# A retention, channel-MLP and attention kernel: other first transfers, matmuls on a constant, and a last value product in halves

## The chip, the cores and the metric

The kernel runs on one core of one Trainium2 chip. The metric is the device time of one execution in microseconds (us), lower is better. The engines are called as the profile calls them: PE is TensorE (PEld its weight loads), ACT is ScalarE, DVE is VectorE, POOL is GpSimd and SP is SyncE, which issues the DMAs.

## The reference, cut

```python
B, H, S, D = 2, 8, 768, 64           # batch, heads, tokens, head width; model width 512
# 1 retention: a decaying state per head
for t in range(S):
    state = gamma * state + outer(k[:, :, t], v[:, :, t])
    y[:, :, t] = q[:, :, t] @ state / sqrt(D)
# 2 channel MLP on the heads put side by side (width 512, hidden 2048)
xn = (x - mean) / sqrt(var + 1e-6) * g_ln
x = x + relu(xn @ w_ch1) @ w_ch2
# 3 four causal attentions of width 64; each token takes its best two by a gate
for e in range(4):
    q, k, v = x @ wq[e], x @ wk[e], x @ wv[e]
    ye = softmax(causal(q @ k.T / 8)) @ v @ wo[e]
    out += (weight of e for the token, or 0) * ye
```

## The kernel before

**Stages.** The tokens of a batch are cut into six tiles of 128, so the retention stage has twelve tiles, taken in the order batch 0, batch 1, batch 0 and so on (`tiles`). The channel stage walks eight blocks `f` of 256 hidden columns, in six of which (`SEVEN`) it forms sums of weights and of activations and multiplies with those (`w_sums`, `m_h7`); its second product is L594, whose results VectorE adds to the residual stream at L597. The attention stage follows (`q_phase`, `a_phase`), for pairs of query tiles `g`.

**One retention tile** (`r_tile`). `load` brings two pairs: `kq`, keys and queries with the head width on the partitions, and `vk`, values and keys with tokens on the partitions, 512 KB each, and for batch 0 a table `tabY` of 256 KB. GpSimd scales the values by the table `tabV` (L414, result `vs`). TensorE makes the scores (L426), VectorE masks them with `caus` (L430, result `am`), TensorE multiplies the masked scores with `vs` (L445), adds the part of the state from the third tile on (L438), and updates the state from `vk` and `vs` (L452), which ScalarE copies to SBUF (L459). The result times `tabY` is transposed with the identity `ident` (L470), normalised and transposed back.

**What sets the order.** Every step is a node of a planner (`Plan`): the engine or engines it may run on with a planned cost, what it reads and writes, and a priority, which is the order of creation plus a bias. `issue` walks planned time: at each moment it looks at the engines in turn and gives a free one the ready step with the lowest priority number whose buffers fit, and that order is what each engine gets. A DMA is a step of the engine "D" and is issued by SyncE, in planned order. A buffer is given the first free place of its kind in planned time (there are four for `kq`, three for `vk`), and on the chip the DMA waits until that place is really free. The two rules in the code:

```python
free = {e: 0.0 for n in self.nodes for e in n.eng}   # engines in the order of first mention
...
for e in free:
    if free[e] > t:
        continue
    for n in sorted(waiting[e], key=lambda n: n.prio):
```

**The end.** For a query tile pair `g` and an expert pair `p`, `a_value` transposes the weighted softmax rows (L879), copies them (L333, where every copy that either ScalarE or VectorE may do is recorded) and multiplies them with the values (L890) for both query tiles at once, 256 columns; ScalarE and VectorE make a high and a low part `at` of it (L896, L897). `a_out` multiplies these with `wo` (L909), six terms per query tile `z`, copies the sums out and writes them (L918). For the last pair the second query tile leaves in two halves that share a bank.

Of the kernel before, what the change touches and what calls it, by code (L numbers as in the profile page):

```python
# [27 lines left out]
AF = mybir.ActivationFunctionType  # L28
OP = mybir.AluOpType
# [3 lines left out]
B, H, S, D = 2, 8, 768, 64  # L33
DM = H * D
FF = 4 * DM
E, HD = 4, 64
C = 128
# [11 lines left out]
NEG = -1000000000.0  # L49
# [162 lines left out]
def retention_channel_mlp_mixture_attention(ctx: ExitStack, tc: tile.TileContext, a):  # L212
    nc = tc.nc
    pe, act, dve, pool, sp = nc.tensor, nc.scalar, nc.vector, nc.gpsimd, nc.sync
# [6 lines left out]
    caus = cst.tile([128, C], F32, name="caus")  # L221
    tabV = cst.tile([128, NC, H], F32, name="tabV")
# [4 lines left out]
    negs = cst.tile([128, C], F32, name="negs")  # L227
    ps = pp.tile([128, 8 * 512], F32, name="ps")
# [27 lines left out]
    f32, f32r, u32 = typed(F32), typed(F32R), typed(U32)  # L256
# [11 lines left out]
    x = o_r  # L268
# [21 lines left out]
    x = o_h - 2 * (4 * KB + 16)  # L290
# [20 lines left out]
    P = Plan()  # L311

    def new(n):
        return Buf(PL[n], n)

    def PE(c, fn, r=(), w=(), hold=()):
        P.add({"T": c}, lambda e: fn(), r, w, lat=0.2, hold=hold)

    def ACT(c, fn, r=(), w=()):
        P.add({"A": c}, lambda e: fn(), r, w)  # L320

    def DVE(c, fn, r=(), w=()):
        P.add({"V": c}, lambda e: fn(), r, w)
# [14 lines left out]
    def act_c(n):  # L338
        return 0.06 + n * 0.84e-3

    def dve_c(n):
        return 0.08 + n * 1.05e-3
# [21 lines left out]
    TY = {}  # L364
# [4 lines left out]
    def load(i):  # L369
        b, c = tiles[i]  # L370
        kq, vk = new("kq"), new("vk")
        n = 2 if i == 0 else 1
        for y in range(n):
            h = slice(1024 // n * y, 1024 // n * (y + 1))
            DMA(512e3 / n, lambda h=h: sp.dma_start(f32(kq)[:, h], a["kq"][b, c][:, h]), w=[(kq, y)])
            if i == 0 and y == 0:
                DMA(24e3, lambda: sp.dma_start(tabV, a["tabV"]), w=["tabV"])
                DMA(64e3, lambda: sp.dma_start(caus, a["caus"]), w=["caus"])
        DMA(512e3, lambda: sp.dma_start(f32(vk), a["vk"][b, c]), w=[vk])
        if b == 0:  # L380
            ty = TY[c] = new("tabY")
            DMA(256e3, lambda: sp.dma_start(f32(ty), a["tabY"][c]), w=[ty])
        L[i] = (kq, vk)

    load(0)
    DMA(64e3, lambda: sp.dma_start(ident, a["ident"]), w=["ident"])
    load(1)
    load(2)
    DMA(2e3, lambda: sp.dma_start(gln, a["gln"]), w=["gln"])
    DVE(0.1, lambda: dve.memset(half, -0.5), w=["half"])  # L390
# [8 lines left out]
    STATE = new("state")  # L399
# [6 lines left out]
    def r_tile(i):  # L406
# [6 lines left out]
        vs = new("vs")  # L413
        POOL(1.15, lambda: pool.tensor_tensor(h3(f32(vs)), h3(v()),  # L414
                                             tabV[:, c, :, None].to_broadcast([128, H, D]), OP.mult),
             r=[vk, "tabV"], w=[vs])
        if c < 2:
            zero_s(SNB[b][c])
        PA, AM = [new("ps") for _ in range(2)], [new("am") for _ in range(2)]
# [28 lines left out]
        if c < NC - 1:  # L448
            def upd():
                for p in range(NP):  # L450
                    for h in range(2):
                        pe.matmul(state(b)[64 * h:64 * h + 64, p * D:(p + 1) * D], lhsT=h3(k())[:, 2 * p + h],  # L452
                                  rhs=h3(f32(vs))[:, 2 * p + h], start=(i == 0 and p == 0), stop=False,
                                  skip_group_check=True)
            PE(0.65, upd, r=[vk, vs] + (["first"] if i == 1 else []), w=[(STATE, b)] + (["first"] if i == 0 else []))
            sn = SN[b] = SNB[b][c % 2]
            for h in range(2):
                hs = slice(64 * h, 64 * h + 64)
                ACT(0.38, lambda h=h, hs=hs: act.activation(  # L459
                    r4(f32(sn))[hs, :, hs], state(b)[hs].rearrange("p (a e) -> p a e", a=NP), AF.Copy),  # L460
                    r=[(STATE, b)], w=[(sn, h)])
# [242 lines left out]
    MW = {}  # L704
# [10 lines left out]
    def mw(n, lo, k, c0, c1):  # L715
        h, l, w = MW[n]
        return f32r(l if lo else h)[:, k * w + c0:k * w + c1]
# [144 lines left out]
        P.bias += (20, 40)[b]  # L862
        return PR

    def a_value(b, g, p, PRS):
# [17 lines left out]
        av = new("psa")  # L883
        for j0 in range(0, nj, 2):
            def mm(j0=j0):
                for j in (j0, j0 + 1):
                    last = j == nj - 1
                    for x in range(2):
                        e = 2 * p + x
                        pe.matmul(f32(av)[64 * x:64 * x + 64, (C if last else 0):2 * C],  # L890
                                  lhsT=f32(VV[b, j])[:, e * HD:(e + 1) * HD],
                                  rhs=f32(PT[x])[:, 2 * j * C:(2 * j + (1 if last else 2)) * C],
                                  start=(j == 0), stop=last, skip_group_check=True)
            PE(0.97 if j0 + 2 < nj else 0.76, mm, r=[VV[b, j0], VV[b, j0 + 1]] + [(pt, j0 // 2) for pt in PT], w=[av])
        at = new("at")
        ACT(act_c(256), lambda: act.activation(f32r(at)[:, :256], f32(av, 256), AF.Copy), r=[av], w=[(at, 0)])  # L896
        DVE(dve_c(256), lambda: dve.tensor_tensor(f32r(at)[:, 256:], f32(av, 256), f32(at)[:, :256], OP.subtract),  # L897
            r=[av, (at, 0)], w=[(at, 1)])
        return at

    def a_out(b, g, ats, last):
        terms = [(p, y, lo) for p in range(2) for y, lo in ((0, 0), (0, 1), (1, 0))]
        pas, obs = [new("psa") for _ in range(2)], [new("ob") for _ in range(2)]

        def part(z, i0, i1, cs):
            def mm():
                for i in range(i0, i1):
                    p, y, lo = terms[i]
                    pe.matmul(f32(pas[z])[:, cs], lhsT=f32r(ats[p])[:, y * 256 + z * C:y * 256 + (z + 1) * C],  # L909
                              rhs=mw("wo", lo, p, cs.start, cs.stop), start=(i == 0), stop=(i == 5),  # L910
                              skip_group_check=True)
            PE(0.22 * (i1 - i0) * (cs.stop - cs.start) / DM, mm,
               r=list(MW["wo"][:2]) + [(ats[p], y) for p, y, lo in terms[i0:i1]], w=[pas[z]])

        def leave(z, cs):
            t0 = (2 * g + z) * C
            COPY(cs.stop - cs.start, lambda: f32(obs[z])[:, cs], lambda: f32(pas[z])[:, cs], [pas[z]], [(obs[z], cs.start)])
# [3 lines left out]
        all_ = slice(0, DM)  # L921
        if last:
            for i0, i1 in ((0, 3), (3, 5)):
                for z in range(2):
                    part(z, i0, i1, all_)
        for z in range(2):
            for cs in (slice(0, DM // 2), slice(DM // 2, DM)) if last and z else (all_,):
                part(z, 5 if last else 0, 6, cs)
                leave(z, cs)

    pieces = [(f, i) for f in range(NFC) for i in ((2, 3, 0, 1) if f in SEVEN else range(NPC))]
    early = {0: (0, 1), 2: (2, 3), 7: (4, 5), 9: (6, 7)}
# [133 lines left out]
```

## Time and profile before

| | us |
|---|---|
| median of three runs | 459.22 (459.13 to 460.65) |
| the profiled execution | 459.39 |
| its span, first to last instruction | 457.3 |
| TensorE busy | 442.7 (97%) |
| VectorE, ScalarE, GpSimd busy | 336.1, 228.4, 208.8 |
| data moved | 40.09 MB |

Times in the views below run from the span's start. A busy time of TensorE includes the pipelined ends of its matmuls. A product of plain float32 operands stands in the trace as two instructions, one that is made of rounded halves as one. "Idle before" in brackets is how long the engine stood still ahead of a row, and what released it.

### The profile page before, as it was taken

How to read it: one execution, taken by the hardware profiler on the slowest of the kernel's cores; microseconds unless marked ns; L12 is line 12 of the kernel's file. 1: busy time of each engine (PE TensorE's matmuls, PEld its weight loads, DVE VectorE, ACT ScalarE, POOL GpSimd, SP SyncE). 2: the span in 40 equal slices, each digit the busy share in tenths (PEclk: the TensorE clock that was granted, in tenths of full speed). 3: DMA queues.
4: the chain of work that ended last, by engine and by line, in shares of the span. 5: the costliest groups of instructions: out<-in, count | busy, mean ns of one | idle time of the engine just before them, and what ended most of it. 6: DMA issues, size and time to landing. Idle time of an engine off the chain costs nothing.

```text
span 457.3 us, 8243 instructions
## 1 busy us (share of the span) xinstructions
PE 442.7 (97%) x3081; PEld 417.1 (91%) x3081; DVE 336.1 (73%) x701; ACT 228.4 (50%) x479; POOL 208.8 (46%) x212
## 2 busy tenths in 40 slices
PE   4999999999999999999999999999999999999996
PEld 3888899999999999999999999999899988898774
DVE  2697885779848959879779677466657988778962
ACT  0686684365246326244354154145534767745852
POOL 1588779879976304323244044007500415224450
PEclk9999999999999999999999999999999999999999
DMA  7899930224103104014022002002220221101111
GB/s 264 315 326 326 345 100 6 94 97 134 46 1 138 48 0 162 24 36 149 1 72 68 1 2 92 1 0 94 69 70 16 63 62 47 47 1 46 49 48 46
DMA packets 14984, 40.09 MB, mean 88 GB/s; under 512 B 2272, under 2 KB 4960, under 8 KB 14944
## 3 DMA queue, kind: packets, MB, share of 16 engines
q1 hardware_dynamic: 14944, 39.57, 25.5%
q8 instruction: 24, 0.39, 0.3%
q14 instruction: 16, 0.13, 0.1%
HBM read 33.27 MB, written 3.15 MB: 80 GB/s over the span
## 4 chain that ended last, share of the span: by engine, by line
PE 80%; DVE 5%; DMA 5%; ACT 3%; issue 3%; POOL 2%; SPq 0%; POOLq 0%; DVEq 0%; ACTq 0%
PE ps L594 25%; PE ps L653 15%; PE ps L575 7%; PE ps L737 6%; PE ps L890 4%; PE ps L879 4%; PE ps L774 4%; PE ps L909 4%; DMA kq<-in_kq_dram 3%; PE ps L837 2%; PE ps L838 2%; DVE sf L546 2%; PE ps L445 2%; PE ps L426 2%; PE ps L470 2%
## 5 line engine op out<-in xcount | busy, mean ns | idle before, releaser
L594 PE MATMUL ps<-h,w 128*128 128x384 f32 x768 | 145.9, 336 | 1.7 <-DVE xT L597 1.4
L594 PEld LDWEIGHTS ps<-h,w 128*128 128x128 f32 x768 | 133.9, 188 | 3.3 <-DVE xT L597 2.7
L597 DVE TENSOR_TENSOR xT<-xT,ps 128x384 f32<-128x384 f32 x128 | 69.3, 550 | 29.1 <-PE ps L594 28.9
L859 POOL TENSOR_SCALAR pr<-pr,sm,gate 128x384 f32<-128x384 f32 (+5 forms) x48 | 34.8, 734 | 81.2 <-DVE ps L844 32.5
L531 POOL TENSOR_TENSOR w<-wy,w 128x512 fp32r<-128x512 f32 x26 | 34.4, 1333 | 56.2 <-PE ps L594 34.8
L653 PE MATMUL ps<-t,S 128*128 128x384 f32 x216 | 43.3, 335 | 0.0
L847 ACT ACTIVATE pr<-ps,sm 128x384 f32<-128x384 f32 (+5 forms) x48 | 30.3, 634 | 16.5 <-DVE sm L845 10.4
L653 PEld LDWEIGHTS ps<-t,S 128*128 128x128 f32 x216 | 38.0, 188 | 0.0
L660 ACT ACTIVATE u<-ps 128x384 f32<-128x384 f32 x36 | 17.5, 487 | 37.8 <-PE ps L653 31.0
L575 PE MATMUL ps<-x,w 128*128 128x384 f32 x192 | 35.0, 336 | 0.0
L506 ACT ACTIVATE wx<-raw 128x512 f32<-128x512 f32 x32 | 21.5, 671 | 23.9 <-DVE ps L510 16.2
L575 PEld LDWEIGHTS ps<-x,w 128*128 128x128 f32 x192 | 33.3, 188 | 0.0
L507 POOL TENSOR_SCALAR wx<-wx 128x512 f32<-128x512 f32 x32 | 20.5, 641 | 26.7 <-ACT wx L506 25.7
L845 DVE TENSOR_REDUCE sm<-ps 128x1 f32<-128x384 f32 (+5 forms) x48 | 30.0, 625 | 2.8
L653 PE MATMUL ps<-x,w 128*128 128x384 f32 x144 | 28.8, 335 | 0.0
L530 ACT ACTIVATE w<-wy 128x512 fp32r<-128x512 f32 x26 | 16.2, 628 | 24.1 <-PE ps L594 18.6
L668 ACT ACTIVATE h<-ps 128x384 fp32r<-128x384 f32 x36 | 17.6, 488 | 18.8 <-PE ps L653 9.4
L653 PEld LDWEIGHTS ps<-x,w 128*128 128x128 f32 x144 | 25.3, 188 | 0.0
L669 DVE SCALAR_TENSOR_TENSOR h<-ps,h 128x384 fp32r<-128x384 f32 x36 | 19.9, 552 | 4.8 <-ACT h L668 4.8
L512 DVE SCALAR_TENSOR_TENSOR wy<-raw,ps 128x512 uint32<-128x512 uint32 x32 | 21.7, 683 | 2.3 <-POOL w L531 1.8
L510 DVE SCALAR_TENSOR_TENSOR ps<-wx,ps 128x512 uint32<-128x512 uint32 x32 | 22.2, 695 | 1.0
L508 DVE TENSOR_SCALAR ps<-wx 128x512 uint32<-128x512 uint32 x32 | 22.0, 688 | 0.8 <-POOL wx L507 0.3
(116 smaller groups left out, 885.2 us busy)
## 6 DMA issues: line engine op xcount, KB each, us to landing
raw<-in_w_dram SPq DMA_DIRECT2D x32, 512.0 KB, 4.0
vk<-in_vk_dram SPq DMA_DIRECT2D x12, 512.0 KB, 5.6
kq<-in_kq_dram SPq DMA_DIRECT2D x11, 512.0 KB, 6.2
qk<-qk SPq DMA_DIRECT2D x32, 96.0 KB, 2.1
out_dram<-ob SPq DMA_DIRECT2D x11, 256.0 KB, 2.0
tabY<-in_tabY_dram SPq DMA_DIRECT2D x6, 256.0 KB, 5.2
vraw<-in_wv_dram SPq DMA_DIRECT2D x1, 520.0 KB, 3.6
kq<-in_kq_dram SPq DMA_DIRECT2D x2, 256.0 KB, 3.0
```

Of the source, the lines that this page charges most:

```text
L508: DVE(0.62, lambda: dve.tensor_scalar(u32(z), u32(x), 4, 1, op0=OP.logical_shift_left, op1=OP.logical_shift_right), r=[x], w=[z])
L510: DVE(0.7, lambda: dve.scalar_tensor_tensor(u32(z), u32(x), 0x80000000, u32(z), op0=OP.bitwise_and, op1=OP.bitwise_or), r=[x, z], w=[z])
L512: DVE(0.7, lambda: dve.scalar_tensor_tensor(u32(y), words(0), 29, u32(z), op0=OP.logical_shift_right, op1=OP.bitwise_or), r=[raw, z], w=[y])
L531: POOL(1.34, lambda: pool.tensor_tensor(f32r(l), f32(y), f32(h), OP.subtract), r=[y, h], w=[l])
L575: pe.matmul(f32(pa, TB), lhsT=wt, rhs=blk(f32r(xt[b][j]))[:, k], start=(n == 0), stop=(n == 11))
L594: pe.matmul(f32(pa, TB), lhsT=wt, rhs=t, start=(n == 0), stop=(n == 5))
L597: DVE(0.55, lambda k=k, pa=pa: dve.tensor_tensor(blk(f32(xt))[:, k], blk(f32(xt))[:, k], f32(pa, TB), OP.add), r=[pa] + keys(xt), w=[(xt, ...
L653: pe.matmul(f32(pa, TB), lhsT=wt, rhs=t, start=(first and n == 0), stop=(n == 5), skip_group_check=True)
L737: pe.matmul(f32(pa, TB), lhsT=mw(n, lo, k, p * 128, (p + 1) * 128), rhs=blk(f32r(xt))[:, k], start=(i == 0), stop=(i == 11))
L845: dve.tensor_reduce(f32(sm)[:, z:z + 1], f32(s, nk), axis=AX, op=OP.max, negate=True)
L847: ACT(act_c(nk) + .18, lambda s=s, pr=pr, z=z: act.activation(f32(pr, nk), f32(s, nk), AF.Exp, bias=f32(sm)[:, z:z + 1], scale=1.0, accum_ ...
L859: POOL(0.28 + nk * 0.95e-3, lambda pr=pr, z=z, e=e: pool.tensor_scalar(f32(pr, nk), f32(pr, nk), f32(sm)[:, 6 + z:7 + z], GT[b, j][:, cc, ...
```

## The change

The tables `caus` and `tabV` are loaded from ScalarE's queue instead of SyncE's. The first `vk` is loaded in two halves, values and keys, and the steps that read them wait for their own half. Tile 1's loads stand ahead of `ident` and of the first `tabY`. The constant `negs` is set at the start, and six matmuls of it with itself into an unused bank are TensorE's first step. At the end, the value product of the last pair of query tiles and the last pair of experts is made in two products of 128 columns, each in a bank of its own, with their copies in halves; the output product of the last pair has its first three terms for all parts ahead of the last three, and each half of the second query tile has its own bank. The planned cost of L909 goes from 0.22 to 0.24.

```diff
         for y in range(n):
             h = slice(1024 // n * y, 1024 // n * (y + 1))
             DMA(512e3 / n, lambda h=h: sp.dma_start(f32(kq)[:, h], a["kq"][b, c][:, h]), w=[(kq, y)])
-            if i == 0 and y == 0:
-                DMA(24e3, lambda: sp.dma_start(tabV, a["tabV"]), w=["tabV"])
-                DMA(64e3, lambda: sp.dma_start(caus, a["caus"]), w=["caus"])
-        DMA(512e3, lambda: sp.dma_start(f32(vk), a["vk"][b, c]), w=[vk])
+        for y in range(n):
+            h = slice(1024 // n * y, 1024 // n * (y + 1))
+            DMA(512e3 / n, lambda h=h: sp.dma_start(f32(vk)[:, h], a["vk"][b, c][:, h]),
+                w=[(vk, y)] if n == 2 else [(vk, 0), (vk, 1)])
         if b == 0:
             ty = TY[c] = new("tabY")
-            DMA(256e3, lambda: sp.dma_start(f32(ty), a["tabY"][c]), w=[ty])
+            if i:
+                DMA(256e3, lambda: sp.dma_start(f32(ty), a["tabY"][c]), w=[ty])
...
+    for name, dst in (("caus", caus), ("tabV", tabV)):
+        P.add({"A": 0.5}, lambda e, name=name, dst=dst: act.dma_start(dst, a[name]), w=[name], lat=3.0)
+    DVE(0.2, lambda: dve.memset(negs, NEG), w=["negs"])
+    idle = new("ps")
+
+    def warm():
+        for z in range(6):
+            pe.matmul(f32(idle)[:, :C], lhsT=negs, rhs=negs, start=True, stop=True)
+    PE(2.2, warm, r=["negs"], w=[idle])
     load(0)
+    load(1)
     DMA(64e3, lambda: sp.dma_start(ident, a["ident"]), w=["ident"])
-    load(1)
+    DMA(256e3, lambda: sp.dma_start(f32(TY[0]), a["tabY"][0]), w=[TY[0]])
     load(2)
...
-             r=[vk, "tabV"], w=[vs])
+             r=[(vk, 0), "tabV"], w=[vs])
...
-            PE(0.65, upd, r=[vk, vs] + (["first"] if i == 1 else []), w=[(STATE, b)] + (["first"] if i == 0 else []))
+            PE(0.65, upd, r=[(vk, 1), vs] + (["first"] if i == 1 else []), w=[(STATE, b)] + (["first"] if i == 0 else []))
...
+        avs, at = [new("psa") for _ in range(2 if last else 1)], new("at")
+        for av, zs in zip(avs, ((0,), (1,)) if last else ((0, 1),)):
+            for j0 in range(0, nj, 2):
+                def mm(j0=j0, zs=zs, av=av):
+                    for j in (j0, j0 + 1):
+                        own = [z for z in zs if z or j < nj - 1]
...
+                PE((0.97 if j0 + 2 < nj else 0.76) * len(zs) / 2, mm,
+                   r=[VV[b, j0], VV[b, j0 + 1]] + [(pt, j0 // 2) for pt in PT], w=[av])
+            cs = slice(zs[0] * C, (zs[-1] + 1) * C)
...
+            ACT(act_c(n), lambda cs=cs, av=av: act.activation(f32r(at)[:, cs], f32(av)[:, cs], AF.Copy),
+                r=[av], w=[(at, 0, z) for z in zs])
...
-            PE(0.22 * (i1 - i0) * (cs.stop - cs.start) / DM, mm,
-               r=list(MW["wo"][:2]) + [(ats[p], y) for p, y, lo in terms[i0:i1]], w=[pas[z]])
+            PE(0.24 * (i1 - i0) * (cs.stop - cs.start) / DM, mm,
+               r=list(MW["wo"][:2]) + [(ats[p], y, z) for p, y, lo in terms[i0:i1]], w=[pa])
...
+        out = [(new("psa"), 0, full), (new("psa"), 1, full)]
         if last:
-            for i0, i1 in ((0, 3), (3, 5)):
-                for z in range(2):
-                    part(z, i0, i1, all_)
-        for z in range(2):
-            for cs in (slice(0, DM // 2), slice(DM // 2, DM)) if last and z else (all_,):
-                part(z, 5 if last else 0, 6, cs)
-                leave(z, cs)
+            out[1:] = [(new("ps"), 1, left), (new("ps"), 1, right)]
+            for o in out:
+                part(*o[:2], 0, 3, o[2])
+        for o in out:
+            part(*o[:2], 3 if last else 0, 6, o[2])
+            leave(*o)
...
-    DVE(0.1, lambda: dve.memset(negs, NEG), w=["negs"])
...
-                ats.append(a_value(b, g, p, PRS))
+                ats.append(a_value(b, g, p, PRS, p == 1 and b == B - 1 and g == gs[-1]))
```

## Rows read from the trace of the kernel before

**Rows 1.** The page's busy times: engine, busy us, share of the span.
```profile
PE 442.7 (97%) x3081; PEld 417.1 (91%) x3081; DVE 336.1 (73%) x701; ACT 228.4 (50%) x479; POOL 208.8 (46%) x212
```
**Rows 2.** The page's slices, DMA engines: busy tenths in 40 slices of the span.
```profile
DMA  7899930224103104014022002002220221101111
```
**Rows 3.** The chain of waits, first 40 us: start, us, what.
```profile
2.57 4.88 DMA vk<-in_vk_dram
...
7.59 1.05 POOL vs L414
...
8.69 1.97 PE ps L445 x16
10.66 0.85 PE ps L452 x16
11.52 1.37 PE ps L426 x16
12.89 0.58 PE ps L470 x4
...
13.77 0.69 PE ps L452 x16
14.46 1.09 PE ps L426 x16
15.55 1.02 PE ps L445 x16
```
**Rows 4.** Waits of TensorE, whole run: us in total, times, longest.
```profile
PE ps L426 <- DMA kq<-in_kq_dram: 4.6, 3, 3.4
PE ps L445 <- POOL vs L414: 2.3, 2, 2.0
PE ps L594 <- DVE xT L597: 1.4, 4, 0.5
```
**Rows 5.** The timeline of SyncE's DMA issues, first 12 us: start, us.
```profile
2.09 0.43 SPq L375 DMA_DIRECT2D kq<-in_kq_dram  x1
2.57 0.43 SPq L379 DMA_DIRECT2D vk<-in_vk_dram  x1
...
4.47 0.43 SPq L379 DMA_DIRECT2D vk<-in_vk_dram  x1
...
11.61 0.33 SPq L379 DMA_DIRECT2D vk<-in_vk_dram  x1
```
**Rows 6.** Busy times in a window; last: granted clock, DMA share, GB/s.
```profile
11.00:13.00 2.00, 2.00 (x28) 1.76 (x27) 0.48 (x2) 1.38 (x2) 1.04 (x1) 1.00 0.42 107
```
**Rows 7.** The timeline of instructions, first 18 us: start, us, instruction.
```profile
5.45 1.23 PE L426 MATMUL ps<-kq 64*128 64x128 f32 x8 [0.81 <-DMA kq<-in_kq_dram]
...
6.71 1.29 DVE L430 TENSOR_TENSOR am<-ps,caus 128x512 f32<-128x512 f32 x2 [4.62 <-PE ps L426]
...
17.00 1.06 PE L438 MATMUL ps<-kq,sn 128*128 128x128 f32 x8
```
**Rows 8.** The DMA issue at 4.47: size, us from issue to landing.
```profile
vk<-in_vk_dram SPq DMA_DIRECT2D x1, 512.0 KB, 6.8
```
**Rows 9.** The chain of waits, last 9 us.
```profile
448.31 2.53 PE ps L890 x24
450.84 2.17 PE ps L909 x9
...
453.03 0.39 ACT ob L333
...
453.46 0.40 PE ps L909
...
453.88 0.42 DVE ob L333
```
**Rows 10.** The timeline of SyncE, last two output issues.
```profile
453.86 0.38 SPq L918 DMA_DIRECT2D out_dram<-ob  x1
...
454.34 0.40 SPq L918 DMA_DIRECT2D out_dram<-ob  x1
```

More of the change, by code (lines that the diff above doesn't have):

```diff
@@ L863, in a_scores, with a_value @@
         return PR
-    def a_value(b, g, p, PRS):
+    def a_value(b, g, p, PRS, last):
         nj = 2 * g + 2
@@ L882, in a_value @@
                      [pa], [(pt, s0 // 4)])
[L883 to L898, printed above, removed]
+        avs, at = [new("psa") for _ in range(2 if last else 1)], new("at")
[4 more added lines that the diff above has]
+                        own = [z for z in zs if z or j < nj - 1]
+                        if not own:
+                            continue
+                        at_z = 0 if j == nj - 1 else own[0]
+                        for x in range(2):
+                            e = 2 * p + x
+                            pe.matmul(f32(av)[64 * x:64 * x + 64, own[0] * C:(own[-1] + 1) * C],
+                                      lhsT=f32(VV[b, j])[:, e * HD:(e + 1) * HD],
+                                      rhs=f32(PT[x])[:, (2 * j + at_z) * C:(2 * j + at_z + len(own)) * C],
+                                      start=(j == 0), stop=(j == nj - 1 - (zs == (0,))), skip_group_check=True)
+                PE((0.97 if j0 + 2 < nj else 0.76) * len(zs) / 2, mm,
+                   r=[VV[b, j0], VV[b, j0 + 1]] + [(pt, j0 // 2) for pt in PT], w=[av])
+            cs = slice(zs[0] * C, (zs[-1] + 1) * C)
+            ls = slice(256 + zs[0] * C, 256 + (zs[-1] + 1) * C)
+            n = C * len(zs)
+            ACT(act_c(n), lambda cs=cs, av=av: act.activation(f32r(at)[:, cs], f32(av)[:, cs], AF.Copy),
+                r=[av], w=[(at, 0, z) for z in zs])
+            DVE(dve_c(n), lambda cs=cs, ls=ls, av=av: dve.tensor_tensor(f32r(at)[:, ls], f32(av)[:, cs], f32(at)[:, cs], OP.subtract),
+                r=[av] + [(at, 0, z) for z in zs], w=[(at, 1, z) for z in zs])
@@ L902, in a_out, with part @@
         terms = [(p, y, lo) for p in range(2) for y, lo in ((0, 0), (0, 1), (1, 0))]
-        pas, obs = [new("psa") for _ in range(2)], [new("ob") for _ in range(2)]
-        def part(z, i0, i1, cs):
+        obs = [new("ob") for _ in range(2)]
+        full, left, right = slice(0, DM), slice(0, DM // 2), slice(DM // 2, DM)
+        def part(pa, z, i0, i1, cs):
             def mm():
@@ L908, in mm, with leave @@
                     p, y, lo = terms[i]
-                    pe.matmul(f32(pas[z])[:, cs], lhsT=f32r(ats[p])[:, y * 256 + z * C:y * 256 + (z + 1) * C],
-                              rhs=mw("wo", lo, p, cs.start, cs.stop), start=(i == 0), stop=(i == 5),
-                              skip_group_check=True)
-            PE(0.22 * (i1 - i0) * (cs.stop - cs.start) / DM, mm,
-               r=list(MW["wo"][:2]) + [(ats[p], y) for p, y, lo in terms[i0:i1]], w=[pas[z]])
-        def leave(z, cs):
+                    pe.matmul(f32(pa)[:, cs], lhsT=f32r(ats[p])[:, y * 256 + z * C:y * 256 + (z + 1) * C],
+                              rhs=mw("wo", lo, p, cs.start, cs.stop), start=(i == 0), stop=(i == 5))
+            PE(0.24 * (i1 - i0) * (cs.stop - cs.start) / DM, mm,
+               r=list(MW["wo"][:2]) + [(ats[p], y, z) for p, y, lo in terms[i0:i1]], w=[pa])
+        def leave(pa, z, cs):
             t0 = (2 * g + z) * C
-            COPY(cs.stop - cs.start, lambda: f32(obs[z])[:, cs], lambda: f32(pas[z])[:, cs], [pas[z]], [(obs[z], cs.start)])
+            COPY(cs.stop - cs.start, lambda: f32(obs[z])[:, cs], lambda: f32(pa)[:, cs], [pa], [(obs[z], cs.start)])
             DMA(512 * (cs.stop - cs.start), lambda: sp.dma_start(a["out"][b, t0:t0 + C, cs], f32(obs[z])[:, cs]),
                 r=[(obs[z], cs.start)], w=[])
-        all_ = slice(0, DM)
+        out = [(new("psa"), 0, full), (new("psa"), 1, full)]
         if last:
-            for i0, i1 in ((0, 3), (3, 5)):
-                for z in range(2):
-                    part(z, i0, i1, all_)
-        for z in range(2):
-            for cs in (slice(0, DM // 2), slice(DM // 2, DM)) if last and z else (all_,):
-                part(z, 5 if last else 0, 6, cs)
-                leave(z, cs)
+            out[1:] = [(new("ps"), 1, left), (new("ps"), 1, right)]
[4 more added lines that the diff above has]
+            leave(*o)
     pieces = [(f, i) for f in range(NFC) for i in ((2, 3, 0, 1) if f in SEVEN else range(NPC))]
```

## The prediction

> **What bounds the kernel now.** I read the page's busy shares first. TensorE is busy 97% of the span [rows 1], so nothing that happens on another engine counts unless TensorE waits for it; what is left to win is where it stands still or runs slowly. The list of TensorE's waits over the whole run shows where that is [rows 4]: 4.6 us for keys and 2.3 us for the scaled values, most of both in the first 9 us, and in the 390 us after the retention stage one kind that counts, 1.4 us in four waits for the residual sum at L597. So I went to the chain of waits at the start [rows 3]: the first value tile is on its way from 2.57 to 7.45, GpSimd scales it until 8.64, and TensorE starts the product with it at 8.69. The same chain shows a second loss. L445's sixteen instructions take 1.97 us there and 1.02 at 15.55; L452's take 0.85 and later 0.69, L426's 1.37 and later 1.09; eight of L426 at 5.45 take 1.23 [rows 7], where 0.55 is half of a later sixteen. The granted clock is written as 1.00 over all of this, in that window too [rows 6], but the durations are twice as long, as at the lower of the two levels (1.2 instead of 2.4 GHz); they go by durations here. TensorE had been working without a gap since 8.69 when they became short, inside the group at 11.52.
>
> The third view is the DMA row of the page [rows 2]: slices of 11.4 us show seven, eight and then three times nine tenths, and three from 57 us on. A start that is earlier on TensorE alone is therefore lent, not given: keys and values have to come earlier too. The windows show the one real hole in the transfers, 11 to 13 us, with a share of 0.42, so 1.17 us of idle transfer time [rows 6]. SyncE's own row says why: the third value tile is issued only at 11.61 [rows 5], as soon as L452 of tile 0 is done (10.66 + 0.85, [rows 3]). The planner takes the first free place, and the place it takes is the one that tile 0 has just left.
>
> The last view is the chain at the end [rows 9]: 24 instructions of the value product, nine of L909, then a copy of 0.39, one more L909 of 0.40 that waited for it, a copy of 0.42, and the last output issued at 454.34 [rows 10].
>
> **The change at the start.** Two issues leave SyncE: the second half of the keys moves from 2.09 to 1.1 (two steps of 0.48, as from 2.09 to 2.57, [rows 5]), the values from 2.57 to 1.6, the keys in row form to 2.1, tile 1's pair to 2.6 and 3.1, since the identity and tabY now go behind them. The tables themselves, 88 KB, still move. The two issues on ScalarE delay nothing: its first step is the state copy (L459), which reads what L452 writes. Landings I interpolate by bytes. Key half two had 600 KB in front of its end and let TensorE go at 5.45 [rows 7]; tile 0's value pair had 1112 KB and landed at 7.45 [rows 3]. That is 0.25 MB per us, so 856 KB (both key halves, tables, values alone) gives 6.4; issued earlier by some 0.4 to 0.9, but sharing with what is close behind it, I take 6.3 (5.6 to 6.5). The keys in row form follow at 7.2. GpSimd then takes 1.05 and some 0.1 of hand-over: scaled values at 7.5, against 8.64.
>
> By the planner's costs the state update (L452) now comes ready 0.2 us ahead of the second mask, so it should stand in front of the masked product (L445). TensorE starts it at 7.5, and the product at 8.1.
>
> **The matmuls on a constant.** Six calls are twelve instructions, as L438's four calls are eight. Eight take 1.06 to 1.09 at the upper level [rows 7], so one takes 0.136, and 0.27 at the lower: 3.3 us from some 1.0 (an estimate; a memset that stands first on VectorE is all that they wait for) to 4.3 at most. Key half one lands at 3.4 (the longest wait for keys, [rows 4]), so the first scores are held for up to 0.9. What hides it: even with all sixteen score instructions at the lower level (2.46) and both masks, 1.29 [rows 7], the masks end at 8.1, just when the update is done. With that cover gone it would cost what is over, at most 0.9. What it may buy: the 0.95 of L445, 0.16 of L452 and 0.28 of L426, 1.4 in all, if the clock is up by 7.5. TensorE would then have worked almost without a gap since 1.0, as it had from 8.69 on before its instructions became short, so I take the gain as given, with nothing as the other end.
>
> Tile 0 with the scores of tile 1 then ends at 7.5 + 0.69 + 1.02 + 1.09, or 10.3, where it was 12.89 [rows 3]: a lead of 2.6. The next thing late is tile 1's value pair. It landed at 4.47 + 6.8 = 11.3 [rows 5, 8]; issued 1.37 earlier with 320 KB less ahead of it I take 10.1. Scaled it is there at 11.2, so TensorE loses 0.9 again. Update 0.69, the transpositions 0.58, product 1.02 and the scores of tile 2, 1.09, end at 14.6; the same set ended at 16.57 (15.55 + 1.02, [rows 3]). The lead is 2.0. The tabY of tile 0, moved behind tile 1's pair, comes at about 11 by the same bytes; its multiplication, a pass like one mask (half of 1.29), ends at 11.7, before the transpositions are due at 11.9. A later tabY would cost what it is late, up to the 0.3 until the product could stand in.
>
> The transfers get: tile 0's place is free after the update, now at about 8.2 instead of 11.5, so the third value pair is issued 3.4 us earlier and the hole of 1.17 is closed; with smaller gaps that the same earlier issues fill (the seven and the eight of the DMA row) 1.4 to 2.0. The lead that stays is the lower of the two, as long as the share is near one: **1.8**, with 0.6 (half the hole) and 3.0 (2.6 and the later waits for keys, 0.4) as ends. What comes after is TensorE at work without a break, and keeps it.
>
> **The change at the end.** The last value product becomes 20 and 24 instructions of 128 columns. The nearest row of that shape (64 weight columns, 128 moving) is L445's 1.02 for 16, 0.064 each [rows 3]: 44 take 2.8 to 2.9 where 24 took 2.53 [rows 9], so TensorE does 0.35 more. The split by halves lets the copies of the first half run under the second. L909 does the same columns in smaller pieces: the nine, 2.17, and the last half, 0.12 (half of a ninth of 2.17), which with a bank of its own no longer waits out a copy (0.39 + 0.04). TensorE ends at 448.31 + 2.88 + 2.17 + 0.12 = 453.5 instead of 453.86. Then a copy of 0.38 or 0.42, so 453.9 instead of 454.30. But SyncE has three outputs to issue, 0.48 apart [rows 10], and the 256 KB one goes first when its copy ends at about 453.4: the last leaves at 454.1 to 454.3. I take **0.25** (a loss of 0.1 to a gain of 0.6).
> The Trainium skill (TensorE: Matmul & The Clock Gate, Back-to-back issue gap) gives about 81 ns per matmul of 128 columns in a sustained stream of loads and matmuls, which speaks against halves. By it 44 would take 3.6 us, and the end would come about 0.4 later than before instead of 0.25 earlier. The row of this kernel with the same shape shows 64 ns, and decides.
>
> **The sum.** 459.39 (the profiled execution; span 457.3, 2.1 around it; the median of the runs is 0.17 lower) - 1.8 - 0.25 = **457.3 us**, 0.45% less. 0.5%, 2.3 us, is about what a measurement of this kernel can tell from no change, so the bound lies at 456.9.
>
> **Rivals.** *The transfers give nothing back.* The DMA row stays at nine after the start [rows 2]; if closing the hole only makes the next transfers queue, the lead shrinks to about 0.6 when TensorE meets the next late keys. For it: landing took 6.8 us with the queue full [rows 8]. Against it: 1.17 us of idle transfer time is real. Time 459.39 - 0.6 - 0.1 = 458.7.
> The Trainium skill (DMA: Bandwidth & Descriptors, Issuing engines are not separate DMA queues) says that issues from several engines run on the same sixteen DMA engines and interleave, so a second issuer saves issue time only. That is this rival for the tables' part, two steps of 0.48; no run so far shows the second issuer here.
>
> *The lead is kept in full.* 2.6 from tile 0 and the later waits for keys (0.4) too, 0.5 at the end: 459.39 - 3.5 = 455.9. For it: a share of 0.9 leaves some 10% of fifty microseconds. Against it: tile 1's values are late again.
>
> *The constant matmuls don't raise the clock.* Then L445 and L452 stay at 1.97 and 0.85; 0.9 of that 1.1 falls into the wait for tile 1's values. About 457.6, inside the forecast.
>
> *Slower: another order in the channel stage.* The planner walks its engines in the order in which steps first name them (`for e in free`). That was the DMA queue first; now ScalarE is named first. Ties, between copies that either ScalarE or VectorE may do and between steps that want the same bank, can fall the other way in all that follows. The place where that would be paid is ahead of L594, where TensorE now waits 0.2 to 0.5 once per weight block, four times 1.4 in all [rows 4]. There are six such blocks with sums. If the weight sums of each come 0.5 later, 3.0 are lost: 460.3. It decides from 0.34 each, and is slower by over 0.5% (461.5) from 0.70. For it: only that the order is replanned; against it: in that stage the plan is paced by TensorE, and a start moved by 2 us moves everything alike.
>
> **How the numbers follow.** Forecast (456.6 to 458.2, its own range) 0.44, half-lost lead (to 459.3) 0.18, full lead 0.28, slower order 0.10, of which 0.06 are past 461.5; that the constant matmuls leave the clock low has 0.25, inside the first two. Faster by over 0.5%: the full lead and 0.17 of the forecast's lower part, 0.45. Slower 0.06, the rest, 0.49, within. The range leaves out the slower order and the best fifth of the full lead: 455.2 to 459.3.
>
> **What would show it.** In the changed profile: the values landing near 6.3 and scaling done by 7.5; L452 ahead of L445 in tile 0; L445 of tile 0 near 1.05 us; the third value pair issued near 8.3; DMA shares near 1 between 11 and 13; the channel stage beginning 1.8 earlier; one copy between the last L909 and the last output. Wrong if the value tile lands no earlier, if the clock is still low at 9 us, if waits for keys take the lead back before 45 us, or if the waits ahead of L594 grow.

## The result, and the profile after

The changed kernel takes 461.46 us (median of 11 runs, 459.97 to 466.06) beside 458.48 for the kernel before (11 runs, 458.08 to 460.65): a ratio of 1.0067, interval 1.0049 to 1.0085. It is slower by about 3 us, where 457.3 was forecast; the range (up to 459.3) does not hold it. The profiled execution took 461.36, span 459.5. One per mille is 0.46 us below.

The page after: busy times, and of the 40 slices the DMA engines and the granted clock.

```profile
PE 445.6 (97%) x3118; PEld 419.6 (91%) x3118; DVE 333.1 (73%) x694; ACT 232.7 (51%) x488; POOL 207.8 (45%) x212
...
PEclk8999999999999999999999999999999999999999
DMA  8999832204103204014021002002220221101111
```

The first two slices of the DMA row are at eight and nine tenths, one tenth more than in [rows 2]. TensorE is still the engine that is never idle for long. Its waits over the whole run, after:

```profile
PE ps L605 <- DVE xT L608: 2.4, 5, 1.0
PE ps L463 <- DMA vk<-in_vk_dram: 2.0, 1, 2.0
PE ps L481 <- DVE xT L475: 1.2, 3, 0.8
PE ps L393 <- DVE negs L388: 1.0, 1, 1.0
PE ps L748 <- DVE qk L767: 0.9, 1, 0.9
PE ps L437 <- ACT xc L501: 0.7, 1, 0.7
...
PE ps L848 <- DVE qk L767: 0.3, 1, 0.3
PE ps L890 <- ACT ob L333: 0.2, 1, 0.2
```

The waits for keys and values of [rows 4] are less than half of what they were, as meant. Part of that is only another name: of the 3.4 us ahead of the first scores, 2.9 are now matmuls on the constant, and those scores start at 4.00 instead of 3.42, though all sixteen are done by 5.45 instead of 6.68. In their place stand others that [rows 4] does not have: the transpositions wait for the product with tabY (L481 for L475), the scores for a normalised tile (L437 for L501), and the residual sum (L605 for L608, L594 for L597 before) has five waits for four, the new one of a whole microsecond.

The start on TensorE, after, and the windows of 7 to 13 us (the last three numbers are the granted clock, 1.00 being the upper of the two levels and 0.50 the lower, the DMA share and GB/s):

```profile
1.03 2.93 PE L393 MATMUL ps<-negs 128*128 128x128 f32 x12 [1.03 <-DVE negs L388]
4.00 1.45 PE L437 MATMUL ps<-kq 64*128 64x128 f32 x16
7.46 0.89 PE L463 MATMUL ps<-vs,vk 128*64 128x64 f32 x16 [2.01 <-DMA vk<-in_vk_dram]
8.09 1.97 PE L456 MATMUL ps<-am,vs 128*64 128x128 f32 x16
9.99 1.72 PE L437 MATMUL ps<-kq 64*128 64x128 f32 x16
11.64 0.69 PE L463 MATMUL ps<-vs,vk 128*64 128x64 f32 x16
```

```profile
7.00:8.00 1.00, 0.54 (x15) 0.57 (x17) 0.00 (x0) 0.00 (x0) 0.00 (x0) 0.89 1.02 410
8.00:9.00 1.00, 1.00 (x16) 1.00 (x14) 0.00 (x0) 0.56 (x1) 0.00 (x0) 0.50 0.99 384
9.00:10.00 1.00, 1.00 (x12) 0.67 (x9) 0.00 (x0) 0.99 (x2) 0.00 (x0) 0.50 1.10 426
10.00:11.00 1.00, 1.00 (x10) 1.00 (x10) 0.00 (x0) 0.49 (x2) 0.76 (x1) 0.50 1.02 416
11.00:12.00 1.00, 1.00 (x23) 0.88 (x22) 0.26 (x1) 0.00 (x0) 0.28 (x1) 0.90 1.03 420
12.00:13.00 1.00, 0.32 (x12) 0.18 (x8) 1.00 (x3) 0.62 (x2) 0.00 (x0) 1.00 1.05 337
```

The constant matmuls did raise the clock: sixteen of L437 take 1.45, where eight took 1.23 before [rows 7]. Then TensorE stands for 2.0 us, and at 8 us the granted clock is 0.50: L456 takes 1.97, as before the change. Tile 0 with the next scores ends at 11.7, not at 10.3. The hole in the transfers from 11 to 13 us is closed.

The order changed as well. The channel stage's first product (L575 before, L586 after): durations, first and last start, first of the kernel before, then after.

```profile
L575 PE MATMUL ps<-x,w x192: 333/335/423, 45.4 to 128.3; 128*128 128x384 f32 x192
```

```profile
L586 PE MATMUL ps<-x,w x192: 333/334/442, 59.2 to 128.4; 128*128 128x384 f32 x192
```

Before, twelve of these stood inside the retention stage, at 45.4; now none comes ahead of 59.2. The new long wait is in the timeline at 109.67, and the chain of waits leads through VectorE there:

```profile
105.32 2.06 DVE L557 TENSOR_TENSOR sf<-wy,wy 128x256 f32<-128x256 f32 x1 [1.63 <-ACT wy L529]
...
109.08 0.54 DVE L608 TENSOR_TENSOR xT<-xT,ps 128x384 f32<-128x384 f32 x1
...
109.67 1.34 PE L605 MATMUL ps<-h,w 128*128 128x384 f32 x6 [1.01 <-DVE xT L608]
```

```profile
105.32 3.83 DVE sf L557 x3
```

The sums of weights (L557) come late on VectorE, the residual sum stands behind them, and TensorE behind that. The end, chain of waits after:

```profile
451.00 2.55 PE ps L905 x44
453.56 2.33 PE ps L929 x15
455.91 0.38 ACT ob L333
```

From the start of the last value product to the span's end it is 8.5 us, 9.0 before [rows 9].

### The profile page after: what moved, and what is told of

It is laid out like the page before. It is cut to its first block, busy times and chain, and to the rows that moved or that the text cites. A ratio compares the mean times of both kernels' runs of the same rounds, so it can differ in the third digit from the quotient of the medians.

```text
span 459.5 us, 8304 instructions
## 1 busy us (share of the span) xinstructions
PE 445.6 (97%) x3118; PEld 419.6 (91%) x3118; DVE 333.1 (73%) x694; ACT 232.7 (51%) x488; POOL 207.8 (45%) x212
## 4 chain that ended last, share of the span: by engine, by line
PE 72%; DVE 12%; ACT 6%; DMA 4%; issue 4%; POOL 1%; SPq 0%; DVEq 0%; POOLq 0%; ACTq 0%
PE ps L605 24%; PE ps L664 14%; PE ps L586 6%; PE ps L748 6%; PE ps L905 4%; PE ps L890 4%; PE ps L785 3%; DVE sf L557 3%; PE ps L929 2%; PE ps L848 2%; PE ps L849 2%; DMA kq<-in_kq_dram 2%; DMA raw<-in_w_dram 1%; DVE wy L523 1%; PE ps L437 1%
## 5 line engine op out<-in xcount | busy, mean ns | idle before, releaser
L605 PE MATMUL ps<-h,w 128*128 128x384 f32 x768 | 146.2, 335 | 2.4 <-DVE xT L608 2.4
L605 PEld LDWEIGHTS ps<-h,w 128*128 128x128 f32 x768 | 133.8, 188 | 4.2 <-DVE xT L608 4.0
L608 DVE TENSOR_TENSOR xT<-xT,ps 128x384 f32<-128x384 f32 x128 | 68.9, 550 | 26.3 <-PE ps L605 26.0
L586 PE MATMUL ps<-x,w 128*128 128x384 f32 x192 | 35.2, 336 | 0.0
L586 PEld LDWEIGHTS ps<-x,w 128*128 128x128 f32 x192 | 33.2, 188 | 0.3 <-issue 0.2
L679 ACT ACTIVATE h<-ps 128x384 fp32r<-128x384 f32 x36 | 17.6, 488 | 19.9 <-PE ps L664 11.7
L441 DVE TENSOR_TENSOR am<-ps,caus 128x512 f32<-128x512 f32 x24 | 15.5, 684 | 12.0 <-PE ps L437 10.2
```

What stands on the lines that cost most here:

```text
L586: pe.matmul(f32(pa, TB), lhsT=wt, rhs=blk(f32r(xt[b][j]))[:, k], start=(n == 0), stop=(n == 11))
L605: pe.matmul(f32(pa, TB), lhsT=wt, rhs=t, start=(n == 0), stop=(n == 5))
L608: DVE(0.55, lambda k=k, pa=pa: dve.tensor_tensor(blk(f32(xt))[:, k], blk(f32(xt))[:, k], f32(pa, TB), OP.add), r=[pa] + keys(xt), w=[(xt, ...
```

## The experiments

A ratio is to the kernel before as it was measured beside each run (458.9 to 459.0 us below, 458.48 beside the change), so ratios compare where times do not. Two landmarks of each trace serve as well: the start of the first query product (L737 before, L748 after, 24 instructions), early in the attention stage (the first key product stands 5.3 us ahead of it), and the start of the last value product. Before: 326.2 and 448.24; after: 327.3 and 450.93. So of the 2.7 us lost by then 1.1 were lost ahead of the first landmark and 1.6 between the two. The first scatters from trace to trace: the run of the end alone, which has the start and the order of before, reaches it at 327.1, so the 1.1 is uncertain by about as much. The distance between the two hardly scatters (below).

**The end alone**, edited as in the change, with the planned cost of L909 left at 0.22; the line that calls for it:

```diff
-                ats.append(a_value(b, g, p, PRS))
+                ats.append(a_value(b, g, p, PRS, p == 1 and b == B - 1 and g == gs[-1]))
```

> The kernel before with the change's end alone (value product in halves, own banks, planned cost of L909 left at 0.22). The built order differs from before in the last value and output products only. Theory O (the loss is order: the steps that were planned anew cost 1.1 us in the retention and channel stages and 1.5 us in the attention stage, and the end gains 0.5): 0.4 to 0.6 us faster than before. Rival T (the end gives nothing, because three output issues in a row on SyncE set it): within 0.1 us of before.

458.72 us, ratio 1.0003 (0.9992 to 1.0014). Between a gain of 0.4 and a loss of 0.6: the 0.4 to 0.6 that was expected lies at the edge or outside, and a gain of 0.25 can be neither shown nor excluded. The traces tell more than the times here. From the second landmark to the span's end it is 9.0 to 9.1 us in the three traces with the old end, 8.8 to 8.9 in the ten with the new end and the ties of before, 8.6 in the three with the new end and the change's ties. SyncE's last three issues start 5.2, 5.0 and 4.9 us behind that landmark (before, this run and the change) and take 1.3 us together in each.

**The ties alone**: the kernel before, engines walked in the order that the change gives.

```diff
-        free = {e: 0.0 for n in self.nodes for e in n.eng}
+        free = {e: 0.0 for e in "AVTDG"}
```

> The kernel before with one line changed: the planner looks at its engines in the order of the changed kernel (ScalarE first), nothing else. The order is the same up to the middle of the channel stage and differs in places from there, most in the attention stage. Theory O: a good part of the 1.5 us of the attention stage, 0.7 to 1.5 us slower than before. Theory D (the loss comes from the start itself, its transfers and its clock): no difference, within 0.2 us.

460.51, ratio 1.0038 (1.0025 to 1.0051): 1.7 us for an edit that adds no work. The landmarks are 325.6 and 449.48: ahead by 0.6 at the first, behind by 1.2 at the second. All of it is lost in the attention stage. Between the landmarks, the kernel before and then this run (behind the window its length and the busy times of TensorE, its weight loads, VectorE, ScalarE and GpSimd):

```profile
326.16:448.24 122.08, 121.67 (x839) 106.87 (x839) 92.83 (x268) 72.63 (x187) 35.92 (x49) 1.00 0.16 47
```

```profile
325.62:449.48 123.86, 122.84 (x839) 106.65 (x839) 90.69 (x262) 75.37 (x193) 35.76 (x49) 1.00 0.16 46
```

VectorE is busy 2.1 us less and ScalarE 2.7 more: copies that either may do have changed engines. TensorE stands still 0.6 us longer, in waits of which the kernel before has there only the second, with 0.2:

```profile
PE ps L837 <- DVE qk L756: 0.3, 1, 0.3
PE ps L837 <- ACT pr L847: 0.3, 1, 0.3
PE ps L879 <- ACT ob L333: 0.2, 1, 0.2
```

The other 1.2 us are a longer busy time of the same 839 instructions, which nothing here splits further. The distance itself is steady: 122.0 to 122.2 in the twelve traces with the ties of before, 123.6 to 124.1 in the four with the change's (this run, the change, and two below).

**The change with the ties as before**, and the cost at 0.22.

```diff
-        free = {e: 0.0 for n in self.nodes for e in n.eng}
+        free = {e: 0.0 for e in "DVGTA"}
```

> The changed kernel with the planner's engine order of before and the planned cost of L909 at 0.22 again, so that the attention stage has the order of before; start and end are those of the change. Theory O: the 1.5 us of the attention stage are back, the 1.1 us of the retention order stay, the end gains 0.5: 0.5 to 1.0 us slower than before. Theory D: still 2 to 3 us slower than before, as the full change.

460.85, ratio 1.0031 (1.0015 to 1.0047). That is 1.4 us, a little more than the 0.5 to 1.0 expected. Half of the loss is gone, as the ties' price says; the wait of 1.0 ahead of L605 stays. What is left comes with the start: by its transfers, or by the order that is planned from it.

**The change in the order of the kernel before**: the plan is made as before, and the first nine DMA issues are put into the change's sequence only when they are written out; ScalarE issues the tables. The masked product of tile 0 stays ahead of the state update.

```diff
+        at = [i for i, (n, e) in enumerate(order) if e == "D"][:9]
+        first = [order[i] for i in at]
+        for i, z in zip(at, (2, 0, 1, 3, 4, 7, 8, 6, 5)):
+            order[i] = first[z]
         for n, e in order:
             n.fn(e)
```

> Start and end of the change put into the plan of before: the tables from ScalarE's queue, the first value tile in two halves, tile 1's pair ahead of the identity and tabY, the matmuls on a constant, the end in halves, but every engine's order elsewhere as before. Theory O: the lead of the start (1.3 us in the changed kernel's first tile) is kept in part and the end gains 0.5: 1.0 to 2.0 us faster than before. Theory D: the lead is lost to the transfers or to the clock even so: between 0.6 us faster (the end alone) and 1 us slower.

458.6, ratio 0.9995 (0.998 to 1.0009). With the first transfers of the change and the old order the loss is gone; the gain of 1 to 2 us that was expected is not there either.

**The same without the constant matmuls** (first diff), and **the same with six more of them** behind tile 0's scores, which keep the clock up until the values are there (second).

```diff
-    for z in range(6):
-        pe.matmul(ps[:, 3584:3712], lhsT=negs, rhs=negs, start=True, stop=True)
```

```diff
+                if i == 0 and y0 == 1:
+                    for z in range(6):
+                        pe.matmul(ps[:, 512:640], lhsT=negs, rhs=negs, start=True, stop=True)
```

> e4 (start and end of the change in the frozen order of before) without the matmuls on a constant. Theory C (the constant matmuls raise the clock, the wait of about 2 us for the scaled values lets it fall again, and the first tile runs at the lower level all the same): the same as e4, within 0.3 us. Rival W (they are worth what the prediction said, the first tile's 1.1 to 1.4 us): 0.7 to 1.4 us slower than e4.

> e4 with six more matmuls on the constant behind the first tile's scores, in a bank that is unused then, so that TensorE works through its wait for the scaled values. Theory C: the clock stays up, the product of tile 0 takes 1.05 instead of 1.6 to 2.0 us, the update 0.65 instead of 0.87 and the next scores 1.1 instead of 1.7: 0.7 to 1.4 us faster than e4. Rival L (the transfers are the limit, a faster first tile only waits longer for tile 1): the same as e4 within 0.3 us.

457.68, ratio 0.9978 (0.9958 to 0.9997), and 457.98, ratio 0.9979 (0.9963 to 0.9995): neither differs from the run with twelve instructions by more than the intervals, nor from the other: held constants are worth no more than none. The held ones do what they were made for. TensorE's timeline of that run:

```profile
7.15 1.09 PE L456 MATMUL ps<-am,vs 128*64 128x128 f32 x16 [0.28 <-POOL vs L422]
8.07 0.63 PE L463 MATMUL ps<-vs,vk 128*64 128x64 f32 x16
8.63 1.16 PE L434 MATMUL ps<-kq 64*128 64x128 f32 x16
11.33 0.66 PE L481 MATMUL ps<-ident,xT 128*128 128x128 f32 x4 [1.53 <-DVE xT L475]
```

Tile 0 with the next scores ends at 9.8, and then 1.5 us are spent waiting for the product with tabY. A tile at full clock is only sooner at the next late transfer.

**The whole change without the constant matmuls.**

```diff
-    idle = new("ps")
...
-    PE(2.2, warm, r=["negs"], w=[idle])
```

> The changed kernel without the matmuls on a constant; the built order of all engines is otherwise that of the changed kernel. Theory C: the same as the changed kernel, 2.5 to 3.3 us slower than before. Rival W: slower still, 3.5 to 4.5 us over before. If the constant matmuls do harm by holding the first scores: under 2.3 us over before.

462.0, ratio 1.0066 (1.0043 to 1.0089), the change's own ratio: they neither make the loss nor hide a gain.

**Tile 1's loads back**: the change with ties as before and cost 0.22, and this.

```diff
     load(0)
-    load(1)
     DMA(64e3, lambda: sp.dma_start(ident, a["ident"]), w=["ident"])
     DMA(256e3, lambda: sp.dma_start(f32(TY[0]), a["tabY"][0]), w=[TY[0]])
+    load(1)
```

> e3 (the change with ties and planned cost as before) with tile 1's loads back behind the identity and tabY of tile 0. The built order of the retention and channel stages is then that of before, but for the state update ahead of the masked product in tile 0. Theory O: the retention stage's loss, 1.1 to 1.7 us, came with the moved loads alone: 1.1 to 1.9 us faster than e3, so 0 to 0.6 us faster than before. Theory D (the start's transfers themselves lose): within 0.5 us of e3.

457.39, ratio 0.9963 (0.9946 to 0.9981), 0.68% less than with the loads in front, more than the 0 to 0.6 us expected, and faster than both kernels. TensorE's clock is as low in tile 0 as in the change (0.50 from 8 to 10 us), and the wait for the first `vk` as long (1.95). What differs, beside an earlier tabY, is the order: the channel stage's first product starts at 43.8 again, and the landmarks are 325.0 and 447.10, 1.2 and 1.1 ahead.

**The change with nothing but that edit.**

> The whole change, with one thing put back: tile 1's loads stand behind the identity and the first tabY again. Every step of the retention stage then has the place that it has in the kernel before, but the order of the channel and attention stages stays that of the change. Theory (two costs, moved loads 3 us and order by ties 1.7 us): the first goes and the second stays, so about 3 us under the change, ratio to before 0.999 to 1.001 (458.5 to 459.4). Rival (the two are one cost, paid in the attention stage whatever the start is): 461 or more, ratio 1.004 to 1.007.

458.85, ratio 1.0006 (0.9994 to 1.0018), 0.61% under the change. Landmarks 324.3 and 448.40: ahead by 1.9 at the first, behind by 0.2 at the second. With the ties of the change the stretch between the landmarks takes 2.0 us more than before, and the difference to the run above is theirs, with the cost of 0.24 for L909: 0.43% here, 0.38% for the ties alone. The two costs add.

**The old order with tabY early**: as the frozen order, with the nine issues permuted otherwise.

```diff
-        for i, z in zip(at, (2, 0, 1, 3, 4, 7, 8, 6, 5)):
+        for i, z in zip(at, (2, 0, 1, 3, 4, 6, 5, 7, 8)):
```

> As the frozen-order run (458.6), every engine in the order of the kernel before, but the identity and tabY are issued ahead of tile 1's pair, not behind it. Theory that the late tabY is a cost by itself: the transposition of tile 0 waits less and the run ends near the best so far, 457.2 to 457.8, ratio about 0.997. Rival, that only the re-planned order of the retention stage costs: 458.4 to 458.8 as the frozen order, ratio about 0.9995.

457.39, ratio 0.9968 (0.9957 to 0.9979). The product with tabY in tile 0, VectorE's timeline with tabY late (the first run in the old order) and early (this one):

```profile
10.45 0.69 DVE L472 TENSOR_TENSOR xT<-ps,tabY 128x512 f32<-128x512 f32 x1 [3.79 <-DMA tabY<-in_tabY_dram]
```

```profile
8.29 0.69 DVE L472 TENSOR_TENSOR xT<-ps,tabY 128x512 f32<-128x512 f32 x1 [1.22 <-PE ps L453]
```

With tabY behind tile 1's pair VectorE waits for the transfer; ahead of it, for TensorE. In the old order the late tabY is worth 0.27% against the first run with it, but only 0.1% against the other two, which lies inside their intervals.

**Tile 1's loads back, with held constants**, by the lines shown for the frozen order, and **without any constants**, by those just shown.

> The best version so far (tile 1's loads back, ties as before, 457.39) with six more matmuls on the constant behind the first scores, which keep TensorE busy until the scaled values are there. Theory that the lower clock in tile 0 is on the path once tabY is early: the first tile is 1.5 to 2 us shorter and some of that stays, 455.9 to 456.9. Rival, that the next late thing (tile 1's values) takes it: 457.2 to 457.6, the same as without.

> The best version (tile 1's loads back, ties as before, ratio 0.9963) without the matmuls on the constant. Theory that they are worth nothing even when tabY is early, because the first scores and the masks lie under the wait for the scaled values: ratio 0.995 to 0.998 (456.6 to 458), the same as with them. Rival, that they pay once tabY is no longer the wait, by the 0.28 that the second scores and by the 0.9 that the product take longer at the lower clock: 0.5 to 1.2 us more, ratio 0.998 to 1.000.

457.25, ratio 0.9964 (0.9951 to 0.9977), and 457.75, ratio 0.9972 (0.9961 to 0.9984), beside 0.9963 with the change's twelve. With tabY early too, the constants are worth nothing that can be measured; the 455.9 to 456.9 expected of the held ones did not come.

**The move alone**: the kernel before, with tile 1's loads ahead of the identity and tabY.

```diff
     load(0)
+    load(1)
     DMA(64e3, lambda: sp.dma_start(ident, a["ident"]), w=["ident"])
-    load(1)
+    DMA(256e3, lambda: sp.dma_start(f32(TY[0]), a["tabY"][0]), w=[TY[0]])
     load(2)
```

> The kernel before with one edit: tile 1's loads ahead of the identity and the first tabY. No split, no constant, tables on SyncE, old end, old ties. Theory that the move is the main cost: 1.5 to 3 us slower than before, ratio 1.003 to 1.007 (460.3 to 462.1). Rival, that the move costs only together with the earlier first values, whose place it competes with: within 0.5 us of before, ratio 0.999 to 1.001.

459.18, ratio 1.0011 (0.9999 to 1.0022). The expectation of 1.003 to 1.007 was wrong. This plan too has the channel stage's first product late (60.2), but its longest wait ahead of the residual sum is 0.5, not 1.0. By the traces this is another order than the change's: the two part in tile 0. So the price is not that of the move as such. It belongs to the order that the move makes together with the other edits, or it shows only where the first values come early, which was the rival; this run does not separate the two.

**The new order with tabY early**: the change with ties as before and cost 0.22, where only the issues of the identity and tabY are put ahead of tile 1's pair when they are written out.

```diff
+        at = [i for i, (n, e) in enumerate(order) if e == "D"][:8]
...
+        for i, z in zip(at, (0, 1, 2, 3, 6, 7, 4, 5)):
```

> As the change with ties as before (ratio 1.0031), every engine in the order that the planner made with tile 1's loads in front, but the identity and tabY are issued ahead of tile 1's pair. Theory that the re-planned order of the retention stage is the larger part of the moved loads' price: the time comes down by no more than the late tabY was worth with the old order (0.1 to 0.3%), ratio 1.000 to 1.003 (459 to 460.3). Rival, that the late tabY is all of it and the new order is harmless: as the two runs with early tabY and old order, ratio 0.996 to 0.998 (457 to 458).

461.12, ratio 1.0053 (1.0036 to 1.0069), beyond what was expected and on the side away from the rival: with the new order an early tabY does not help at all (1.0031 with it late). The traces of the two have the same order on every engine. Old and new order with the same first transfers differ by 0.85%, 3.9 us. The windows of 16 to 60 and 106 to 112 us (TensorE's busy time is the second number), new order, then old:

```profile
16.00:60.00 44.00, 41.56 (x553) 36.73 (x553) 34.34 (x67) 30.71 (x57) 35.43 (x46) 1.00 0.87 305
106.00:112.00 6.00, 5.00 (x29) 4.68 (x28) 5.95 (x8) 3.14 (x6) 3.41 (x4) 1.00 0.43 139
```

```profile
16.00:60.00 44.00, 43.21 (x566) 38.12 (x566) 35.45 (x69) 31.73 (x60) 34.90 (x44) 1.00 0.89 319
106.00:112.00 6.00, 6.00 (x36) 6.00 (x36) 5.93 (x10) 1.81 (x3) 6.00 (x5) 1.00 0.28 91
```

TensorE stands still 2.44 us of the retention stage with the new order and 0.79 with the old, and 1.00 against nothing at 106 to 112, in the same wait of 1.0 ahead of the residual sum as in the change. These 2.65 us are nearly the 3.0 by which the two reach the attention stage apart (327.9 and 324.9).

## Why the prediction was wrong

**The step that failed** is "What comes after is TensorE at work without a break, and keeps it", with the argument beside it that "a start moved by 2 us moves everything alike". A lead is kept only by an order that is kept. With the new start and the order of before, eight traces reach the first landmark at 323.5 to 325.3, where the kernel before has 326.2; with the new start and the new order of the retention stage, four reach it at 326.9 to 327.9. Where the ties are those of before as well, the lead is the same at the last value product, within 0.1. The change was planned anew twice over, and each plan costs what the start brings:

| | ratio to before |
|---|---|
| the change's start and end, order and ties of before, tabY early | 0.9963 to 0.9968 |
| the order of the retention stage that is planned with tile 1's loads in front | + 0.0061 to 0.0085 |
| engines named in another order, paid in the attention stage | + 0.0038 to 0.0043 |
| the change | 1.0067 |

Two of the signs of being wrong that were named came: the clock was low at 9 us (0.50), and the waits ahead of the channel stage's second product grew, from 1.4 to 2.4.

**The rival that came true in kind** was the slower one. It was given 0.10, its mechanism, the order of first mention, is shown by the second run, but its place was wrong: it is paid in the attention stage and not ahead of L594. The new wait that stands there, where the rival looked for it, comes from the moved loads, which the rival did not name: changing the sequence of loads changes every planned time after it. That a plan paced by TensorE is safe from this was assumed; the trace of before, in which the channel stage's first product fills a place in the retention stage, could have shown that the plan had a place to lose.

**The transfers.** The values landed at 5.3 (6.3 forecast) and were being scaled from 5.50; the keys in row form at 7.3 (7.2), and L463 started at 7.46 (7.5), ahead of L456 as said. The third value pair was issued at 8.44 (8.3), and the shares from 11 to 13 are 1.03 and 1.05. All of this was right, and better than right for the values: after the change it is the keys that TensorE waits for.

**The clock.** "I take the gain as given" failed. The clock was up by the second scores, but 2.0 us of standing still took it down again, so the first tile gained 1.2 instead of 2.6. The case "the constant matmuls don't raise the clock" was right in its effect and wrong in its reason. It was also right that this would not decide: with the clock held (0.9979) nothing came of it beside the run without constants (0.9978).

**tabY** came at 10.9 ("about 11"), but "before the transpositions are due" was wrong: in the change the product with it starts at 12.35, behind a mask of tile 1 that the new order puts first, and TensorE waits 0.8 for it. The scores of tile 2 end at 15.9, where the same set ended at 16.57: of the lead of 2.0 that was added up to here, 0.7 was there.

**The end** was right in its limit and mis-sized in a term. 44 instructions of 128 columns took 2.55 us, 58 ns each where 64 were taken, so TensorE was done 0.7 sooner instead of 0.36. But the three issues on SyncE come behind it, as the prediction said, and with the ties of before the profile's end is 0.2 to 0.3 shorter, the 0.25 that was forecast; only with the change's ties is it 0.5. In time it is below what the runs can tell. The Trainium skill (TensorE: Matmul & The Clock Gate, Back-to-back issue gap), whose 81 ns spoke against halves, is not borne out by this stream.

**The sum.** The forecast for a kept order, 457.3, is what the runs with that order and tabY early measured (457.25 to 457.75), though from a base 0.4 higher than theirs: the gain was 1.2 to 1.7, not 2.05. That the figures meet is in part luck.

**What stays open.** That the new order is dear is shown, by two runs with the same first transfers; which of its moved steps makes it so is not isolated. The first channel product that leaves the retention stage is the most visible, but the run with the move alone has that too and loses little. The 0.24 for L909 was not run by itself; the parts above leave nothing for it that their intervals would show.

## What to carry to other kernels

In a kernel whose order a planner makes, an edit of the first microsecond is an edit of all that follows: compare the two orders before any sum, and price an order change by itself, by keeping the old order and by changing nothing else. Two edits that looked like housekeeping, which engine is named first and which load stands ahead of a small table, cost more here than the start could bring. And time gained ahead of a late transfer is not gained until the transfer is earlier too.

## What the hardware showed beyond that

In the changed kernel TensorE's granted clock fell to 0.50, the lower of its two levels (1.2 GHz), by 8 us, after 2.0 us of standing still, although twelve instructions on a constant and sixteen of scores stood ahead; with twelve more behind the scores it stayed at 1.00, and L456 took 1.09 instead of 1.97. The record of before says 1.00 where the same product takes 1.97, and so does that of the run without constants and with tile 1's loads back (1.95): durations decide.

The tables from ScalarE's queue stand in a queue of their own in the page's list (packets, MB, share):

```profile
q10 hardware_dynamic: 288, 0.09, 0.1%
```

`caus` landed 3.5 us after its issue there, at 0.7, and 2.7 us after its issue on SyncE, at 1.6: 4.2 and 4.3 from the span's start. What the second issuer saves is the issue steps of the queue that it leaves: the values are issued at 1.63 instead of 2.57. The Trainium skill (DMA: Bandwidth & Descriptors, Issuing engines are not separate DMA queues) says so, and the trace agrees: the transfer itself was no faster.
